# One of VectorE's three shifted arrays made by GpSimd in halves, in a fused attention and SwiGLU kernel

## The chip, the cores and the metric

The kernel runs on one core of a Trainium2 chip. A core has five engines, each with a queue of its own that runs in order: TensorE (PE, matrix products into PSUM), VectorE (DVE, elementwise work), ScalarE (ACT, exponentials and tanh), GpSimd (POOL, elementwise work on SBUF) and SyncE (SP, which here only issues DMAs). Engines meet through semaphores. The metric is the device time of one execution in microseconds (us); runs are repeated and the median is taken.

## The reference

One sequence of 2048 tokens, 512 channels. Multi-head attention with 32 heads of 16 channels and a SwiGLU feed-forward of width 1792 share the input and are mixed by a gate per token:

```
x = A_x                                              # 1 x 2048 x 512, bfloat16
g = sigmoid((x * gate_w).sum(-1, keepdims=True))
q, k, v = split(x @ wqkv)                            # 32 heads of 16
p = softmax(q k^T * 16 ** -0.5)                      # 32 x 2048 x 2048
a = (p v) @ wo
b = (silu(x @ w_gate) * (x @ w_up)) @ w_down
out = g * a + (1 - g) * b
```

The 32 x 2048 x 2048 = 134 million exponentials are what makes the kernel long.

## The kernel before

The scores are cut into 32 units (4 query blocks of 512 by 8 groups of 4 heads), each of 16 key blocks of 128. One key block of one unit is a tile: four heads, 128 keys by 512 queries each. Each tile's exponentials are made by one of two engines.

*By ScalarE.* `emit_pair` puts the scores of two heads (two matmuls that run side by side on different rows of TensorE) into one of two PSUM slots, `s_t`, and an ACTIVATE of 128 x 1024 with Exp writes `e_t`. A slot is free again when its exp has read it. A tile takes two such pairs.

*By VectorE.* `emit_d` lets one or two further score matmuls ride in the same round of TensorE, on rows that the pair leaves free, into a PSUM bank `d_t` (there are three such banks, which the other products share). `first` turns one head's scores into the bit pattern of an approximate exponential, a multiply and add that is stored as uint16 (128 x 512, the group `c_t<-d_t`); four of them make an array `y` of 128 x 2048. One such array is too coarse, so several are summed, and the sum is taken by the product with V. There are two ways. With `groups[n]` = 4, three further arrays are y plus one of three constants (`copy`, 128 x 2048 uint16, `SHIFTS`), four arrays in all. With `groups[n]` = 2, two bit operations (`bits`) and a multiplication (`product`, the TENSOR_TENSOR of 128 x 2048) make two arrays out of y. `quad` decides between them: 4 is taken when the planner has found idle time on TensorE of `SPARE` us. Arrays live in seven buffers ("homes"), which `home` hands out.

`pv` multiplies an array (or a tile's two `e_t`) with V: four matmuls of 512 columns on different columns of TensorE side by side, accumulated in the bank `o_ps`. All work of TensorE is of two modes: rows side by side (scores, "R") or columns side by side (the products with V, the projections and the feed-forward, "C"). Four or fewer matmuls that run side by side are called a round.

Everything else (projections, gate, feed-forward, output) is cut into chains of single rounds and is put between the exps by a `Pacer` with due times.

The order of every engine's instructions is fixed when the program is built. A planner keeps a time for each engine (`plan.pe`, `plan.act`, `plan.dve`), adds a cost for each instruction that it emits, and decides by these times what comes next. `spend` adds to TensorE's time, `spend_v` and `pay` to VectorE's. The main loop (`while au < UNITS`) looks at the room until the next `s_t` slot is free (`s_end`) and fills it with a product with V or a piece of a chain, else it emits the next pair. `fill_dve` does the same for VectorE: array pieces from PSUM that are due (`d_wait`), evictions (`owed`), and array work from SBUF to SBUF (`vops`). How many tiles go to VectorE comes out of this order: `v_unit` gives VectorE another tile when it could have it done in time. GpSimd works only at the start (clearing and filling constants).

All recorded instructions of TensorE carry the line of one helper (L164), those of ScalarE L167, those of VectorE and the DMAs L176, so groups are told apart by tile names.

Of the kernel before, what the change touches and what calls it, by code (L numbers as in the profile page):

```python
# [79 lines left out]
def kernel(  # L80
# [98 lines left out]
    queue = Ordered(nc.sync)  # L179

# [108 lines left out]
    class Plan:  # L289
        pe = dve = act = 0.0  # L290
# [11 lines left out]
    def spend(mode, mms, ready=0.0):  # L302

        plan.seq += 1
        work_at.append((plan.pe, mms))
        plan.pe = max(plan.pe + (0.1 if mode != plan.mode else 0.0), ready) + (0.226 if mode == "F" else 0.223) * mms
        plan.mode = mode

# [15 lines left out]
    def pay(i=0):  # L324
        ready, cost, f, c, key = owed.pop(i)
        spend_v(cost, ready, key)
# [21 lines left out]
    def m_tile(name):  # L348
# [3 lines left out]
        plan.pe = max(plan.pe, banks[i])  # L352
        banks[i] = None
        held[i] = ps_m[i].tile([P, QBW], F32, tag=f"m{i}", name=name)
        return held[i]
# [240 lines left out]
    def gate_end():  # L596
        act(out=ge[:, :], in_=ge[:, :], func=ACT.Exp, scale=-1.0)
        plan.act += 0.2
# [6 lines left out]
        later(0.5, end, plan.act + 0.2)  # L605
# [18 lines left out]
    w_gate, w_up, gs_of = {}, {}, {}  # L624
# [9 lines left out]
    def gu_chain(i):  # L634

        def gated(up):
            vec.scalar_tensor_tensor(out=mt[:, FS[i][1], :], in0=gs_of.pop(i)[:], scalar=0.5, in1=up[:, :],
                                     op0=ALU.mult, op1=ALU.mult)
            m_free(up, plan.dve)

        def gate(gp):
            th = work.tile([P, QBW], BF16, tag="th", name="th")
            flush_act(plan.pe + 0.4)
            act(out=th[:], in_=gp[:, :], func=ACT.Tanh, scale=0.5)
            plan.act = max(plan.act, plan.pe + 0.25) + 0.48
# [6 lines left out]
            later(0.6, f, plan.act + 0.25)  # L652

        cs = slice(FS[i][0] * QBW, (FS[i][0] + 1) * QBW)
        return [columns(DC, "gu", lambda dc, w=w: w[i][:, dc, :], lambda dc: xT[:, dc, cs], end)
                for w, end in ((w_gate, gate), (w_up, lambda p: later(0.6, lambda: gated(p))))]
# [34 lines left out]

    s_end = [0.0, 0.0]
# [4 lines left out]
    def emit_pair(bs, ride=0):  # L697
        i = pairs[0] % 2
        plan.pe = max(plan.pe + (0.1 if plan.mode != "R" else 0.0), s_end[i])
# [7 lines left out]
        for k in ride:  # L707
            emit_d(k)
        spend("R", 1)
        flush_act()  # L710
        ready = plan.pe + 0.27

        def exp():
            act(out=e_t[:], in_=s_t[:], func=ACT.Exp, scale=inv_sqrt_dh)
            plan.act = max(plan.act, ready) + ACT_US
            s_end[i] = plan.act + 0.2
            for b in bs:
                e_end[b] = plan.act + 0.27
        exps.append((ready, exp))
        for b in bs:  # L720
            e_left[b] = pairs[0]
        pairs[0] += 1

    exps = []
    ACT_US = 0.906
# [38 lines left out]
    def emit_d(i, rows=32):  # L764
# [7 lines left out]
        d_t = m_tile("d_t")  # L772
# [33 lines left out]
    def copy(n, k, i, y):  # L806
        h, c = home()
        vec.tensor_scalar(out=c, in0=y, scalar1=SHIFTS[k - 1], scalar2=None, op0=ALU.add)
        ready(n, k, h, c)
        if k == 3:  # L810
            drop(i, plan.dve + 0.2)
            y_live[0] -= 1

# [24 lines left out]
    def pay_v():  # L838
        cost, f, key, _, _ = vops.pop(0)
        spend_v(cost, 0.0, key)  # L840
        f()

    def fill_dve():

        while plan.dve <= plan.pe + 0.2:
            now = plan.dve
            due = [k for k, o in enumerate(owed) if o[0] <= now + 0.05]
            free = [k for k in due if owed[k][4] is None or owed[k][4] != plan.last]
            fit = bool(vops) and vops[0][3] // KT <= closed + AHEAD and c_ready() <= now
# [12 lines left out]
            elif fit:  # L862
                pay_v()
            elif d_wait or owed or vops and vops[0][3] // KT <= closed + AHEAD:
                t = min([w[0] for w in d_wait] + [o[0] for o in owed[:1]]
                        + [c_ready()] * bool(vops and vops[0][3] // KT <= closed + AHEAD))
                if t > plan.pe:
                    break
                plan.dve = max(plan.dve, t)
# [19 lines left out]
    def pv(n, k=None):  # L889

        un = n // KT
        if un not in o_of:
# [9 lines left out]
        if k is not None:  # L902
            c, slot = copies.pop((n, k))
        for i, b in enumerate(range(4 * n, 4 * n + 4)):
            j = HEADS[i]
            c0 = (4 * UNIT[un][1] + j) * VC
            mm(o[32 * j:32 * j + 32, :], lhsT=vaug[:, n % KT, c0:c0 + 32],
               rhs=e_of.pop(b) if k is None else c[:, i * QBW:(i + 1) * QBW],
               start=first, stop=last, tile_position=(0, 32 * j), skip_group_check=True)
            e_left.pop(b, None)  # L910
# [3 lines left out]
        spend("C", 1, 0.0 if k is not None else max(e_end.pop(b, 0.0) for b in range(4 * n, 4 * n + 4)))  # L914
# [194 lines left out]
    plan.dve = plan.pe + 3.9  # L1109

# [22 lines left out]
    def q0_again(p):  # L1133
# [4 lines left out]
        def scale():  # L1138
            act(out=ratio, in_=shift, func=ACT.Exp, scale=inv_sqrt_dh)
            plan.act += 0.48  # L1140
# [162 lines left out]
    def pv_list(now):  # L1303
# [14 lines left out]
        return r if early else [(n, k) for ready, n, k in vready if n // KT == un and (now is None or ready <= now and v_done(n))] + r  # L1318

    def emit_pv(item):  # L1320
        nonlocal closed
        un = closed
        pv(*item)
# [37 lines left out]
    def side(most):  # L1361
# [12 lines left out]
        if t is None or t > plan.pe or 0.226 * mms + (0.1 if plan.mode != mode else 0.0) > most:  # L1374
            return None
# [7 lines left out]
    def next_pv():  # L1383
        flush_act()
        while not pv_list(None):
            if d_wait:
                pay_d()
            elif vops and c_ready() < 1e9:
                pay_v()
            elif owed:  # L1390
# [9 lines left out]
    SLACK = 0.1  # L1400
    LEAD, LAST = 8.0, 6.0
    TILE_US = 1.87
# [31 lines left out]
    def quad():  # L1434
        if spare[0] > SPARE:
            spare[0] = 0.0
            return False
        return True

    def want_d():  # L1440
# [4 lines left out]
        open_ = sum(b is not None and b <= plan.pe for b in banks)  # L1445
# [4 lines left out]
    while au < UNITS:  # L1450
# [5 lines left out]
        back = pairs[0] - min(e_left.values(), default=pairs[0])  # L1456
        if back >= EB - 1:
# [3 lines left out]
        if room > 0.02:  # L1461
            n_pv = pv_list(plan.pe)
            switch = 0.0 if plan.mode == "C" else 0.1
# [3 lines left out]
            urgent = c is not None and c.deadline < 0 and back < EB - 4  # L1467
            visit = len(n_pv) + (len(c.pieces) - c.i if col else 0)
            going = col and 0 < c.i and len(c.pieces) < 6 and back < EB - 3
            if n_pv and fits > 0 and not urgent and not going and (plan.mode == "C" or visit > 1 and fits > 1 and (pv_turn[0] or c is None or col)  # L1470
                                      or back >= EB - 4 or (c is None or col) and fits == 1):
# [28 lines left out]
    while closed < UNITS or vops or vcur:  # L1500
# [26 lines left out]
    assert not vops and not vready and not vcur and not d_wait and not copies and au == closed == UNITS  # L1527
# [62 lines left out]
```

## Time and profile before

| | us |
|---|---|
| median of 3 runs | 773.16 (772.71 to 773.71) |
| profiled execution, its own time | 773.5 |
| its span (first to last instruction) | 771.7 |
| busy: TensorE / VectorE / ScalarE / GpSimd | 734.8 / 731.7 / 756.6 / 10.6 |
| exps of 128 x 1024 on ScalarE | 786 |
| tanh of 128 x 512 on ScalarE | 56, 40.9 busy |

[...] In the groups, the columns after the shapes are count, busy us and mean ns, then the idle time of the engine in front of the group and what ended it. In the waits: us in total, times, longest.

### The profile page before, as it was taken

To read this page: it belongs to the slowest core of one execution; us is meant where nothing else is said; L and a number is where in the kernel's file an instruction comes from. 1 tells how busy PE (TensorE), PEld (TensorE's weight loads), DVE (VectorE), ACT (ScalarE), POOL (GpSimd) and SP (SyncE) were. 2 spreads that over 40 slices of the span, in tenths; PEclk is the share of its full clock that TensorE was granted. 3 is DMA by queue.
4 is the path that set the end of the run, shared out by engine and by line. 5 is a ranking of instruction groups with operands and counts; after the bars stand their busy time and mean duration, and the time that the engine had idled before them with its cause. 6 is when DMAs were issued, how large, how long until landed. Compare 5 with 4: busy or idle time off the path is not lost.

```text
span 771.7 us, 21635 instructions
## 1 busy us (share of the span) xinstructions
PE 734.8 (95%) x8852; PEld 219.4 (28%) x8853; DVE 731.7 (95%) x1192; ACT 756.6 (98%) x855; POOL 10.6 (1%) x25
## 2 busy tenths in 40 slices
PE   8999999998999999999999999999999999999997
PEld 3322222222222222232222222222222232222222
DVE  6789999999989999999999999999999999999994
ACT  5999999999999999999999999999999999999996
POOL 5000000000000000000000000000000000000000
PEclk9999999999999999999999999999999999999999
DMA  8011303043210012220200221302000232100001
GB/s 191 2 19 39 69 16 77 21 122 85 48 43 12 14 41 64 65 46 21 50 15 15 51 72 36 75 21 55 19 12 25 61 78 58 30 19 11 16 28 35
DMA packets 91019, 34.36 MB, mean 45 GB/s; under 512 B 75488, under 2 KB 90472, under 8 KB 90920
## 3 DMA queue, kind: packets, MB, share of 16 engines
q1 hardware_dynamic: 89192, 32.66, 17.8%
q8 instruction: 69, 1.13, 0.6%
q10 hardware_dynamic: 1728, 0.33, 0.2%
q14 instruction: 30, 0.25, 0.1%
HBM read 21.55 MB, written 2.35 MB: 31 GB/s over the span
## 4 chain that ended last, share of the span: by engine, by line
ACT 45%; PE 34%; issue 11%; DVE 9%; DMA 0%; ACTq 0%; DVEq 0%
ACT e_t L167 42%; PE s_t L164 12%; PE o_ps L164 9%; DVE c_t L176 5%; PE gu L164 4%; ACT th L167 3%; PE ops L164 3%; PE qp L164 2%; PE vp L164 1%; PE kp L164 1%; PE dps L164 1%; DVE kaug L176 1%; DVE mt L176 1%; DVE gs L176 1%; PE warm L164 1%
## 5 line engine op out<-in xcount | busy, mean ns | idle before, releaser
L167 ACT ACTIVATE e_t<-s_t 128x1024 bf16<-128x1024 f32 x786 | 735.7, 1152 | 1.2 <-PE s_t L164 1.0
L176 DVE TENSOR_SCALAR c_t<-d_t 128x512 uint16<-128x512 f32 x396 | 262.6, 686 | 10.3 <-PE d_t L164 8.9
L164 PE MATMUL s_t<-qx,kaug 32*128 32x512 bf16 (+1 forms) x1240 | 241.7, 382 | 21.5 <-ACT e_t L167 19.3
L164 PEld LDWEIGHTS <-kaug 32*128 32x128 bf16 (+1 forms) x2048 | 95.7, 91 | 339.3 <-issue 335.4
L164 PE MATMUL o_ps<-e_t,vaug 128*32 128x512 bf16 x1572 | 152.3, 386 | 0.1
L164 PE MATMUL d_t<-qx,kaug 32*128 32x512 bf16 x392 | 138.5, 384 | 0.0
L176 DVE TENSOR_SCALAR c_t<-c_t 128x2048 uint16<-128x2048 uint16 x193 | 130.0, 688 | 0.8
L164 PE MATMUL o_ps<-c_t,vaug 128*32 128x512 bf16 x1096 | 101.9, 385 | 0.5 <-DVE osb L176 0.2
L164 PEld LDWEIGHTS <-vaug 128*32 128x32 bf16 (+1 forms) x2856 | 61.8, 94 | 99.7 <-issue 92.1
L164 PE MATMUL gu<-xT,wg 128*32 128x512 bf16 x896 | 72.4, 384 | 0.0
L176 DVE TENSOR_TENSOR c_t<-c_t 128x2048 bf16<-128x2048 bf16 x59 | 71.9, 1218 | 0.0
L164 PE MATMUL gu<-xT,wu 128*32 128x512 bf16 x896 | 69.2, 383 | 0.1
L164 PE MATMUL ops<-wd_t,mt 128*32 128x512 bf16 x672 | 56.4, 382 | 0.0
L176 DVE TENSOR_SCALAR kaug<-d_t 128x512 uint16<-128x512 f32 x72 | 48.0, 686 | 2.7 <-PE d_t L164 2.7
L164 PE MATMUL s_t<-q,kaug 32*128 32x512 bf16 (+1 forms) x196 | 38.2, 382 | 5.0 <-ACT e_t L167 4.6
L167 ACT ACTIVATE th<-gu 128x512 bf16<-128x512 f32 x56 | 40.9, 731 | 0.0
L176 DVE SCALAR_TENSOR_TENSOR gs<-th,gu 128x512 bf16<-128x512 bf16 x56 | 38.3, 683 | 2.7 <-ACT th L167 2.6
L176 DVE SCALAR_TENSOR_TENSOR mt<-gs,gu 128x512 bf16<-128x512 bf16 x56 | 38.3, 684 | 1.6
L164 PEld LDWEIGHTS <-mt 128*32 128x32 bf16 (+1 forms) x1037 | 24.4, 95 | 27.9 <-issue 21.9
L176 DVE TENSOR_SCALAR c_t<-kaug 128x2048 uint16<-128x2048 uint16 x43 | 29.1, 689 | 0.1
L164 PEld LDWEIGHTS <-wu 128*32 128x32 bf16 x896 | 18.9, 95 | 25.5 <-issue 17.4
L164 PEld LDWEIGHTS <-wg 128*32 128x32 bf16 x896 | 17.6, 94 | 24.9 <-issue 21.7
(141 smaller groups left out, 439.9 us busy)
## 6 DMA issues: line engine op xcount, KB each, us to landing
wg<-in_B_w_gate_dram SPq DMA_DIRECT2D x56, 128.0 KB
wu<-in_B_w_up_dram SPq DMA_DIRECT2D x56, 128.0 KB
on<-osb SPq DMA_DIRECT2D x120, 16.0 KB
rb<-rr SPq DMA_DIRECT2D x15, 128.0 KB
wd_t<-in_B_w_down_dram SPq DMA_DIRECT2D x7, 256.0 KB
qx<-qst SPq DMA_DIRECT2D x96, 16.0 KB
qx<-aq SPq DMA_DIRECT2D x96, 16.0 KB
out_dram<-o_t SPq DMA_DIRECT2D x12, 128.0 KB
```

Source lines behind the costliest of these rows:

```text
L164: return ordered(nc.tensor.matmul(*args, **kw))
L167: ordered(nc.scalar.activation(*args, **kw))
L176: return lambda *a, **kw: ordered(f(*a, **kw))
```

## The change

Of an array set with `groups[n]` = 4, the third shifted array is no longer queued in `vops` when a new list `gq` has a place (two at most). Its work is done in two halves of 1024 columns by `g_half`, either on GpSimd or on VectorE. `g_now` runs whenever VectorE's next instruction is chosen: if at least two (`GNEED`) reads of PSUM are waiting for VectorE, it emits a half on GpSimd, with a wait on the VectorE instruction emitted last. Until the planned end of that half (`plan.lock`), `fill_dve` holds back operations from SBUF to SBUF: those of `vops`, and entries of `owed` that cost under 0.45 (`wide`). When VectorE has nothing else, `g_dve` does a half there.

```diff
+                todo[n] = 3
-                for k in range(1, 4):
+                for k in range(1, 4 - (len(gq) < GQ)):
                     vops.append((0.6, lambda k=k: copy(n, k, h, y), ("y", n) if k == 1 else None, n, True))
+                if len(gq) < GQ:
+                    gq.append([n, h, y, [0, 1], None])
...
+    def g_half(engine, now):
+        g = gq[0]
+        n, h, y, left, c = g
+        if c is None:
+            c = g[4] = home()
+        half = left.pop(0)
+        cols = slice(half * GHALF, (half + 1) * GHALF)
+        before = last_of.get(nc.vector.engine)
+        ins = engine.tensor_scalar(out=c[1][:, cols], in0=y[:, cols], scalar1=SHIFTS[2], scalar2=None, op0=ALU.add)
+        if engine is gps:
+            if before is not None:
+                tc.add_manual_dep(ins.ins, before.name,
+                                  mybir.DependencyInfo(mybir.DependencyClass.Sync, mybir.DependencyReason.DATA),
+                                  reason="beside reads of PSUM")
+            t = plan.pool = plan.lock = max(plan.pool, now + 0.12) + 1.13
+        else:
+            t = plan.dve
+        if not left:
+            gq.pop(0)
+            vready.append((t + 0.3, n, 3))
+            copies[n, 3] = (c[1].bitcast(BF16), c[0])
+            copied(n, h, t)
+
+    def g_now(now):
+        while gq and gq[0][0] // KT <= closed + AHEAD and plan.pool <= now + 0.1 and (gq[0][4] is not None or min(c_free) <= now):
+            soon = sum(d[0] <= now + 0.05 + 0.6 * i for i, d in enumerate(d_wait)) + sum(o[0] <= now + 0.05 and not wide(o[1]) for o in owed)
+            if soon < GNEED:
+                return
+            g_half(gps, now)
+
+    def g_dve():
+        if gq[0][4] is None:
+            plan.dve = max(plan.dve, min(c_free))
+        spend_v(0.335, plan.lock)
+        g_half(vec, plan.dve)
```

A product with V may be cut by columns: where the room in front of the next slot is too short for a whole round, `pv` takes as many quarters of the 512 columns as fit, and the rest comes first at the next chance.

```diff
-    def pv(n, k=None):
+    def pv(n, k=None, most=QBW):
...
+        c0 = cut.pop("done", 0)
+        c1 = min(QBW, c0 + most)
+        cols = slice(c0, c1)
...
+        share = (c1 - c0) / QBW
+        if c1 < QBW:
+            cut.update(item=(n,) if k is None else (n, k), done=c1)
+            spend("C", share, 0.0 if k is not None else max(e_end[b] for b in range(4 * n, 4 * n + 4)))
+            return
...
+            part_cols = int((room + SLACK - switch) / 0.217 * CUTS) * QBW // CUTS
+            if n_pv and plan.mode == "C" and part_cols > 0 and may_cut():
+                emit_pv(n_pv[0], part_cols)
+                continue
```

Four arrays instead of two are taken in more cases, and the planner's figures are set anew (those not shown change in the same way: the tanh, the gate's exps, and the banks that a riding score may take):

```diff
-        plan.pe = max(plan.pe + (0.1 if mode != plan.mode else 0.0), ready) + (0.226 if mode == "F" else 0.223) * mms
+        plan.pe = max(plan.pe + (FLIP if mode != plan.mode else 0.0), ready) + (0.226 if mode == "F" else 0.217) * mms
...
-        ready = plan.pe + 0.27
+        ready = plan.pe + 0.38
...
-            s_end[i] = plan.act + 0.2
+            s_end[i] = plan.act + SLOT
             for b in bs:
-                e_end[b] = plan.act + 0.27
+                e_end[b] = plan.act + 0.06
...
+    FLIP = 0.107
+    SLOT = 0.05
-    ACT_US = 0.906
+    ACT_US = 0.9167
...
-        d_wait.append((plan.pe + 0.5, first, n))
+        d_wait.append(((end[0] if end else plan.pe) + 0.28, first, n))
...
     def quad():
-        if spare[0] > SPARE:
+        if sum(f < 1e9 for f in c_free) < FREE4:
+            return True
+        if spare[0] > SPARE or EAGER(len(GQL()), back[0]):
             spare[0] = 0.0
             return False
         return True
+    FREE4 = 2
+    EAGER = lambda q, b: q == 0 and b <= 4
...
-    SLACK = 0.1
+    SLACK = 0.16
+    CUTS = 4
...
-    TILE_US = 1.87
+    TILE_US = 1.9
```

(In `quad`, False means four arrays.) What the two programs contain, where they differ:

| | before | after |
|---|---|---|
| exps of 128 x 1024 (ScalarE) | 786 | 774 |
| tiles on VectorE: four arrays / two | 41 / 78 | 61 / 64 |
| pieces of 128 x 512 from PSUM (VectorE) | 476 | 500 |
| operations on a whole array of 2048, one input (VectorE) | 279 | 250 |
| products of 2048 (VectorE) | 78 | 64 |
| half copies of 1024: VectorE / GpSimd | 0 / 0 | 23 / 99 |
| products with V, in full rounds | 713 | 759 |
| of them cut in two | 0 | 55 |
| changes of mode on TensorE | 1509 | 1503 |

More of the change, by code (lines that the diff above doesn't have):

```diff
@@ L325, in pay @@
         ready, cost, f, c, key = owed.pop(i)
-        spend_v(cost, ready, key)
+        spend_v(cost, max(ready, plan.lock) if wide(cost) else ready, key)
         keep, plan.chain = plan.chain, None
@@ L604, in end @@
             vec.reciprocal(odds[:, :], ge[:, :])
-        later(0.5, end, plan.act + 0.2)
+        later(0.5, end, plan.act + 0.05)
     def turn_odds():
@@ L651, in f @@
                 gs_of[i] = gs
-            later(0.6, f, plan.act + 0.25)
+            gs_at[i] = plan.act + 0.05
+            later(0.6, f, gs_at[i])
         cs = slice(FS[i][0] * QBW, (FS[i][0] + 1) * QBW)
         return [columns(DC, "gu", lambda dc, w=w: w[i][:, dc, :], lambda dc: xT[:, dc, cs], end)
-                for w, end in ((w_gate, gate), (w_up, lambda p: later(0.6, lambda: gated(p))))]
+                for w, end in ((w_gate, gate), (w_up, lambda p: later(0.6, lambda: gated(p), max(plan.pe + 0.25, gs_at[i]))))]
     scaled = set()
@@ L698, in emit_pair @@
         i = pairs[0] % 2
-        plan.pe = max(plan.pe + (0.1 if plan.mode != "R" else 0.0), s_end[i])
+        plan.pe = max(plan.pe + (FLIP if plan.mode != "R" else 0.0), s_end[i])
         plan.mode = "R"
@@ L706, in emit_pair @@
             e_of[b] = e_t[:, k * QBW:(k + 1) * QBW]
[L707 to L708 removed]
         spend("R", 1)
         flush_act()
[L711 removed]
+        ready = plan.pe + 0.38
+        for k in ride:
+            emit_d(k, riding=True)
         def exp():
@@ L771, in emit_d @@
         left.remove(i)
-        d_t = m_tile("d_t")
+        end = []
+        d_t = m_tile("d_t", end if riding else None)
         score(d_t[:, :], 4 * n + i, rows)
@@ L809, in copy, with copied @@
         ready(n, k, h, c)
-        if k == 3:
-            drop(i, plan.dve + 0.2)
-            y_live[0] -= 1
+        copied(n, i, plan.dve)
+    def copied(n, i, t):
+        todo[n] -= 1
+        if not todo[n]:
+            drop(i, t + 0.2)
+            y_live[0] -= 1
+    todo = {}
+    gq = []
+    GQ = 2
+    GHALF = NV * QBW // 2
+    def g_half(engine, now):
[13 more added lines that the diff above has]
+            t = plan.pool = plan.lock = max(plan.pool, now + 0.12) + 1.13
+        else:
+            t = plan.dve
[10 more added lines that the diff above has]
+            g_half(gps, now)
+    GNEED = 2
+    def g_dve():
[3 more added lines that the diff above has]
+        g_half(vec, plan.dve)
     def bits(n, k, y):
@@ L839, in pay_v @@
         cost, f, key, _, _ = vops.pop(0)
-        spend_v(cost, 0.0, key)
+        spend_v(cost, plan.lock, key)
         f()
@@ L846, in fill_dve @@
             now = plan.dve
-            due = [k for k, o in enumerate(owed) if o[0] <= now + 0.05]
+            g_now(now)
+            shut = locked(now)
+            due = [k for k, o in enumerate(owed) if o[0] <= now + 0.05 and not (shut and wide(o[1]))]
             free = [k for k in due if owed[k][4] is None or owed[k][4] != plan.last]
-            fit = bool(vops) and vops[0][3] // KT <= closed + AHEAD and c_ready() <= now
+            fit = bool(vops) and not shut and vops[0][3] // KT <= closed + AHEAD and c_ready() <= now
             if fit and vops[0][3] // KT < au and vops[0][2] != plan.last:
@@ L863, in fill_dve @@
                 pay_v()
+            elif gq and not shut and gq[0][0] // KT <= closed + AHEAD and (gq[0][4] is not None or min(c_free) <= now) and (len(gq) == GQ or not d_wait):
+                g_dve()
             elif d_wait or owed or vops and vops[0][3] // KT <= closed + AHEAD:
-                t = min([w[0] for w in d_wait] + [o[0] for o in owed[:1]]
-                        + [c_ready()] * bool(vops and vops[0][3] // KT <= closed + AHEAD))
+                t = min([w[0] for w in d_wait] + [max(o[0], plan.lock if wide(o[1]) else 0.0) for o in owed[:1]]
+                        + [max(c_ready(), plan.lock)] * bool(vops and vops[0][3] // KT <= closed + AHEAD))
                 if t > plan.pe:
                     break
-                plan.dve = max(plan.dve, t)
+                plan.dve = max(plan.dve + 0.03, t)
                 plan.last = None
@@ L902, in pv @@
         if k is not None:
-            c, slot = copies.pop((n, k))
+            c, slot = copies[n, k]
         for i, b in enumerate(range(4 * n, 4 * n + 4)):
             j = HEADS[i]
-            c0 = (4 * UNIT[un][1] + j) * VC
-            mm(o[32 * j:32 * j + 32, :], lhsT=vaug[:, n % KT, c0:c0 + 32],
-               rhs=e_of.pop(b) if k is None else c[:, i * QBW:(i + 1) * QBW],
+            v0 = (4 * UNIT[un][1] + j) * VC
+            e = e_of[b] if k is None else c[:, i * QBW:(i + 1) * QBW]
+            mm(o[32 * j:32 * j + 32, cols], lhsT=vaug[:, n % KT, v0:v0 + 32], rhs=e[:, cols],
                start=first, stop=last, tile_position=(0, 32 * j), skip_group_check=True)
-            e_left.pop(b, None)
+        share = (c1 - c0) / QBW
[3 more added lines that the diff above has]
+            return
+        cut.clear()
+        if k is not None:
+            copies.pop((n, k))
+        else:
+            for b in range(4 * n, 4 * n + 4):
+                e_of.pop(b)
+                e_left.pop(b, None)
         pvs[un] += 1
@@ L913, in pv @@
             later(0.6, take_part, plan.pe + 0.47)
-        spend("C", 1, 0.0 if k is not None else max(e_end.pop(b, 0.0) for b in range(4 * n, 4 * n + 4)))
+        spend("C", share, 0.0 if k is not None else max(e_end.pop(b, 0.0) for b in range(4 * n, 4 * n + 4)))
         if k is None:
@@ L1317, in pv_list, with may_cut, emit_pv @@
         r = [(n,) for n in r]
-        return r if early else [(n, k) for ready, n, k in vready if n // KT == un and (now is None or ready <= now and v_done(n))] + r
-    def emit_pv(item):
+        r = r if early else [(n, k) for ready, n, k in vready if n // KT == un and (now is None or ready <= now and v_done(n))] + r
+        item = cut.get("item")
+        return r if item is None else [item] + [i for i in r if i != item]
+    def may_cut():
+        return closed and pvs[closed] and pv_left(closed) > 3
+    def emit_pv(item, most=QBW):
         nonlocal closed
         un = closed
-        pv(*item)
+        pv(item[0], item[1] if len(item) > 1 else None, most)
+        if cut:
+            return
         if len(item) > 1:
@@ L1373, in side @@
         t = m_ready(int(takes)) if takes else 0.0
-        if t is None or t > plan.pe or 0.226 * mms + (0.1 if plan.mode != mode else 0.0) > most:
+        if t is None or t > plan.pe or 0.226 * mms + (FLIP if plan.mode != mode else 0.0) > most:
             return None
@@ L1389, in next_pv @@
                 pay_v()
+            elif gq and (gq[0][4] is not None or min(c_free) < 1e9):
+                g_dve()
             elif owed:
@@ L1444, in want_d @@
         one = c is not None and c.pieces[c.i][2] and (pace.credit > 0 or c.deadline <= plan.slot + 4)
-        open_ = sum(b is not None and b <= plan.pe for b in banks)
+        open_ = sum(b is not None and b <= max(plan.pe, s_end[pairs[0] % 2]) + BANK_WAIT for b in banks)
         if not d_wait and len(vops) < 2:
@@ L1455 @@
         flush_act(plan.pe)
-        back = pairs[0] - min(e_left.values(), default=pairs[0])
-        if back >= EB - 1:
+        back[0] = pairs[0] - min(e_left.values(), default=pairs[0])
+        if back[0] >= EB - 1:
             next_pv()
@@ L1462 @@
             n_pv = pv_list(plan.pe)
-            switch = 0.0 if plan.mode == "C" else 0.1
+            switch = 0.0 if plan.mode == "C" else FLIP
             fits = int((room + SLACK - switch) / 0.216)
@@ L1466 @@
             col = c is not None and (c.pieces[c.i][3:] or "C")[0] == "C"
-            urgent = c is not None and c.deadline < 0 and back < EB - 4
+            urgent = c is not None and c.deadline < 0 and back[0] < EB - 4
             visit = len(n_pv) + (len(c.pieces) - c.i if col else 0)
-            going = col and 0 < c.i and len(c.pieces) < 6 and back < EB - 3
+            going = col and 0 < c.i and len(c.pieces) < 6 and back[0] < EB - 3
             if n_pv and fits > 0 and not urgent and not going and (plan.mode == "C" or visit > 1 and fits > 1 and (pv_turn[0] or c is None or col)
-                                      or back >= EB - 4 or (c is None or col) and fits == 1):
+                                      or back[0] >= EB - 4 or (c is None or col) and fits == 1):
                 emit_pv(n_pv[0])
@@ L1526 @@
         pay()
-    assert not vops and not vready and not vcur and not d_wait and not copies and au == closed == UNITS
+    assert not vops and not gq and not vready and not vcur and not d_wait and not copies and au == closed == UNITS
     assert not at
```

34 lines of the change are left out of this document (24 added, 10 removed).

## The prediction

> **What bounds the kernel now.** I read the page's busy table first, then the chain, the costliest groups, and the waits.
>
> ```profile
> span 771.7 us, 21635 instructions
> ...
> PE 734.8 (95%) x8852; PEld 219.4 (28%) x8853; DVE 731.7 (95%) x1192; ACT 756.6 (98%) x855; POOL 10.6 (1%) x25
> ...
> ACT 45%; PE 34%; issue 11%; DVE 9%; DMA 0%; ACTq 0%; DVEq 0%
> ...
> L167 ACT ACTIVATE e_t<-s_t 128x1024 bf16<-128x1024 f32 x786 | 735.7, 1152 | 1.2 <-PE s_t L164 1.0
> L176 DVE TENSOR_SCALAR c_t<-d_t 128x512 uint16<-128x512 f32 x396 | 262.6, 686 | 10.3 <-PE d_t L164 8.9
> ...
> L176 DVE TENSOR_SCALAR c_t<-c_t 128x2048 uint16<-128x2048 uint16 x193 | 130.0, 688 | 0.8
> ...
> L176 DVE TENSOR_TENSOR c_t<-c_t 128x2048 bf16<-128x2048 bf16 x59 | 71.9, 1218 | 0.0
> ```
>
> Three engines are nearly full, but only ScalarE (ACT) is never without work: its 786 exps show 1.2 us of idle in front of them. The waits say the same from the other side, and a stretch of the timeline shows the beat:
>
> ```profile
> PE s_t L164 <- ACT e_t L167: 24.9, 71, 0.8
> ...
> ACT e_t L167 <- PE s_t L164: 1.0, 3, 0.5
> ```
>
> ```profile
> 302.86 7.55 ACT L167 ACTIVATE e_t<-s_t 128x1024 bf16<-128x1024 f32 x8
> ...
> 306.91 0.39 PE L164 MATMUL s_t<-qx,kaug 32*128 32x512 bf16 x2
> ...
> 307.23 0.62 PE L164 MATMUL o_ps<-e_t,vaug 128*32 128x512 bf16 x8
> ...
> 307.78 0.39 PE L164 MATMUL s_t<-qx,kaug 32*128 32x512 bf16 x2
> ```
>
> TensorE (PE) waits for ScalarE 71 times, 24.9 us; ScalarE waits for TensorE 3 times, 1.0 us. An exp's record is 1.152 long but overlaps the next: eight take 7.55, so (7.55 - 1.15)/7 = 0.914 from start to start. Over the trace's 727 exp-to-exp steps the starts are 0.920 apart in the mean and 0.904 in the median, which is also the least. The excess, 727 x 0.016 = 11.5 us, is exps that start a little late because their scores came late. The first exp starts at 13.6 and the last ends at 763.6: the end of the kernel is the sum of those steps plus 8.1 us of tail. So the term that counts is the number of exps.
>
> **The change, part by part.** Counts are those of the two built programs.
>
> *ScalarE.* 786 exps become 774; tanh stays at 56. Twelve steps of 0.920 fall out: -11.0 us, if the mean lateness stays. Without any lateness the 774 exps need 774 x 0.904 + 56 x 0.478 (the step from a tanh to the next exp) = 726.5 us, before 737.3.
>
> *TensorE.* The 12 pairs of key blocks (six tiles of four) go to VectorE, and more of VectorE's tiles use four arrays instead of two: 61 of 125 after, 41 of 119 before. Each array is one more product with V, four matmuls of 512 columns side by side, one round. Rounds of this kind go from 1650 to 1696, counted in full widths. A round is 0.217 by the trace's steps within a run; the stretch above (one score round, two rounds, the next score) is 0.87 = 3 x 0.217 + 2 changes of mode, so 0.109 a change. Sum: +46 x 0.217 = +10.0; 12 score rounds less, -2.6; 1503 changes of mode instead of 1509, -0.7: +6.7 us. The 55 products cut into 384 and 128 columns (or the like) are priced by the nearest row, the four 128-column rounds of the tail:
>
> ```profile
> 765.53 0.41 PE L164 MATMUL rps<-ident,rt 128*32 128x128 bf16 x16
> ```
>
> They start 0.055 to 0.066 apart, a quarter of 0.217 (0.054): a cut costs 0 to 0.012, 0.7 us at most; I take 0. TensorE's rounds and mode changes were 1650 x 0.217 + 786 x 0.217 + 1509 x 0.109 = 693 us under ScalarE's 737.3 and become 700 under 726.5. It stays below, but the margin falls from 44 to 27 us. That margin is what hides the +6.7; without it they would all be on the path.
>
> *VectorE.* The steps from start to start in the trace are 0.601 for an array piece from PSUM (`c_t<-d_t`), 0.599 for a whole copy of 2048, 1.134 for a product, 0.199 for 512 columns from SBUF (`aq<-qst`), so about 0.33 for 1024. 24 more pieces: +14.4; 29 copies less: -17.4; 14 products less (78 to 64): -15.9; 23 half copies that remain here: +7.7. Sum -11.2. Count times lower-decile step, summed over all kinds, was 715 us and becomes 704; the tail's stretch included, VectorE runs from 0.9 to 768.4.
>
> *GpSimd.* New are 99 adds of a constant on 1024 uint16 columns (the rest of 61 third arrays), each behind a wait on the VectorE instruction emitted before it. What is queued behind such a wait on GpSimd is only the next half; TensorE's product with that array waits for it, and VectorE when it overwrites a buffer. No row shows this operation. The nearest are these:
>
> ```profile
> L508 POOL MEMSET q<- 128x1024 bf16 x1 | 1.0, 954 | 0.0
> ...
> L260 POOL TENSOR_SCALAR_AFFINE_SELECT ident<-ident 128x128 bf16<-128x128 bf16 x1 | 0.3, 292 | 0.0
> ...
> L276 POOL MEMSET sel_t<- 128x4 bf16 x1 | 0.1, 104 | 0.0
> ```
>
> The memset writes 1024 columns but reads nothing: lower end 0.95. The select reads, compares and writes 128 in 0.292, of which 0.104 is the fixed part: 0.104 + 8 x 0.188 = 1.61 for 1024, upper end. An add with one input is nearer to the memset, with a read stream beside the write: I take 1.1.
>
> Does a half hold up VectorE? No row of this trace shows the two together (GpSimd is idle after the start-up). Bounds: nothing, or all VectorE work from SBUF to SBUF stands still until the half is done. I take the second. In the built program 44 of the 99 halves are followed by two VectorE reads of PSUM before the next SBUF-to-SBUF operation, 30 by three or more, 23 by one, 2 by none; a read covers 0.60. With 0.1 to start, 1.1 holds for 1.2: 2 x 1.2 + 23 x 0.6 = 16 us of standing (12.5 at 0.95; 51 at 1.61; 0 without a hold). VectorE then has 704 + 16 = 720 us in a stretch of some 756, before 715 in 767: idle 36 instead of 52. That idle is the cover; it holds.
>
> [...]
>
> *The planner's figures* (mode change 0.1 to 0.107, round 0.223 to 0.217, exp 0.906 to 0.9167, tanh, and when scores, slots and arrays are ready) set the order only. From the end of a pair's score round to the reuse of its slot they add up to 0.27 + 0.906 + 0.2 = 1.376 before, 0.38 + 0.917 + 0.05 = 1.347 after. In the trace an exp that follows at once starts 0.49 after its last score matmul's start (0.27 after the round), and slots are taken 1.10 to 1.20 after the exp's start: about 1.39. Bounds: -0.03 x 774 = 23 us of TensorE standing before a slot, all within its 27 us of margin; or, where the order fits better, up to the 11.5 us of lateness saved. I take 0. SP's queue keeps its 584 entries and nothing is moved past a DMA.
>
> Sum: 771.7 - 11.0 = 760.7 span; the profiled execution's own 773.5 becomes 762.5. The median 773.16 lies 0.3 lower, so **762.1 us**, -1.4%. A measurement of this kernel tells 0.2% (1.5 us) from no change.
>
> **Rivals.**
>
> 1. *GpSimd too slow, so VectorE becomes the bound (slower).* With a half of length L held for h = L + 0.1, the standing is 2h + 23(h - 0.6) + 44(h - 1.2) for h up to 1.8. VectorE's 704, that, and the idle it cannot fill (first 50 us: 12; last 22 us: 11; from the stretch table) make 771.7 when the standing is 45 us: h = 1.61, L = 1.51. From there each 0.1 us costs 7 us: 780 at 1.61, 795 at 1.8. For: the select's row reaches 1.61, and 25 halves have one cover or none. Against: the memset at 0.95. A harder form: every VectorE operation stands still for each half, 99 x 1.1 = 109, so 704 + 109 + 23 = 836. [...] Together 0.23, of which 0.03 for the harder form.
>
> 2. *TensorE too tight.* Lateness grows as its margin shrinks: 11.5 x 44/27 = 18.7, +7.2, so 769. For: the margin; against: no score was late by more than 0.5 us before. 0.14.
>
> 3. *The new figures make TensorE stand before slots* with its other work behind it, and the gain is spent: 12 us of the 23 reach the exps, 773. For: 1.347 against 1.39; against: the margin. 0.06.
>
> 4. *The order fits better.* Half of the lateness goes: 11 + 5.8, so 756. For: the round and mode figures now equal the trace's 0.217 and 0.109, and cuts of 128 columns fill the 0.035 between 0.87 and 0.904; against: lateness is spread evenly over the span (0.6 to 1.0 us in every 50), which names no single fault. 0.07.
>
> That the change does nothing is excluded by the counts.
>
> **How the numbers follow.** Forecast 0.50 (757 to 767), rival 1 0.23, 2 0.14, 3 0.06, 4 0.07. Faster by over 0.2%: 0.50 + 0.14 + 0.07 = 0.71; same 0.06; slower 0.23. The range reaches from rival 4's middle, 755, to 782, past the length of 1.61: below is left out some 0.03, above some 0.12.
>
> **What would show it.** Right: 774 exps, 0.915 to 0.925 from start to start; ScalarE's idle before exps still 1 to 2 us; halves of 0.95 to 1.3 us; copies of 2048 mostly at 0.69 with a few tens stretched by half a microsecond; VectorE's busy share not above 96%. Wrong: exps that wait for TensorE by many microseconds; halves of 1.5 us or more, or PSUM reads stretched beside them; waits of TensorE for `c_t` made by GpSimd.

## The result, and the profile after

The changed kernel takes 826.4 us (824.0 to 829.1, 5 runs) against 773.0 (772.6 to 773.7): a ratio of 1.069 with an interval of 1.067 to 1.071. 762.1 was forecast, 755 to 782 the range. Chance 0.23 stood on the slower side.

The page of the changed kernel, its lines that answer to those before:

```profile
span 824.7 us, 22621 instructions
...
PE 759.3 (92%) x9256; PEld 221.7 (27%) x9257; DVE 749.3 (91%) x1196; ACT 756.0 (92%) x843; POOL 296.2 (36%) x124
...
PE 38%; DVE 29%; POOL 16%; ACT 11%; issue 5%; DMA 1%; POOLq 0%; SPq 0%; DVEq 0%; ACTq 0%
...
L167 ACT ACTIVATE e_t<-s_t 128x1024 bf16<-128x1024 f32 x774 | 729.3, 1066 | 54.2 <-PE d_t L164 26.5
L176 POOL TENSOR_SCALAR c_t<-c_t 128x1024 uint16<-128x1024 uint16 x79 | 227.6, 2888 | 421.5 <-DVE c_t L176 252.8
L176 DVE TENSOR_SCALAR c_t<-d_t 128x512 uint16<-128x512 f32 x428 | 281.1, 681 | 29.2 <-PE d_t L164 25.9
...
L164 PE MATMUL o_ps<-c_t,vaug 128*32 128x512 bf16 (+2 forms) x1352 | 132.0, 375 | 37.4 <-POOL c_t L176 34.2
...
L176 DVE TENSOR_SCALAR c_t<-c_t 128x2048 uint16<-128x2048 uint16 (+1 forms) x189 | 136.6, 736 | 1.9 <-PE o_ps L164 0.6
```

The row that decides is GpSimd's: a half takes 2.89 us in the mean (least 2.76, median 2.77), where 1.1 was counted. The other rows follow from it, as the experiments show. TensorE's products with V stand idle for 34.2 us, waiting for arrays of GpSimd; before, they waited for VectorE alone, and hardly at all:

```profile
L164 PE MATMUL o_ps<-c_t,vaug 128*32 128x512 bf16 x1096 | 101.9, 385 | 0.5 <-DVE osb L176 0.2 <-DVE c_t L176 0.2
```

ScalarE, which had stood 1.2 us before its exps, stands 54.2. In the chain ScalarE falls from 45% to 11% and GpSimd appears with 16%. No engine is full any more: 92, 91 and 92%. They wait for one another in turn.

The sum, from the first exp to the last: 750.0 us before, 802.4 after. Twelve steps of 0.904 less are -10.8. The excess of the exps' steps over 0.904 grows from 11.5 to 69.9, +58.4 (the mean step is 1.002 where 0.920 was forecast); the step from a tanh to the next exp grows from 0.478 to 0.568, 56 of them, +5.0. Together +52.6, measured +52.4.

One such place, in the timeline of the changed kernel (start, length, what; in brackets idle time in front and what ended it):

```profile
296.53 6.06 POOL L176 TENSOR_SCALAR c_t<-c_t 128x1024 uint16<-128x1024 uint16 x2 [5.24 <-DVE c_t L176]
...
300.45 0.38 PE L164 MATMUL o_ps<-c_t,vaug 128*32 128x512 bf16 x2
302.64 0.51 PE L164 MATMUL o_ps<-c_t,vaug 128*32 128x512 bf16 x2 [1.82 <-POOL c_t L176]
...
303.09 0.60 PE L164 MATMUL s_t<-q,kaug 32*128 32x512 bf16 x2
...
303.77 0.69 DVE L176 TENSOR_SCALAR kaug<-d_t 128x512 uint16<-128x512 f32 x1 [2.07 <-PE d_t L164]
303.80 1.02 ACT L167 ACTIVATE e_t<-s_t 128x1024 bf16<-128x1024 f32 x1 [2.21 <-PE d_t L164]
```

Two halves of one array take 6.06 us. TensorE does two of the four matmuls of its product at 300.45 (their columns are in the first half) and waits 1.82 for the others. All later scores stand behind them in its queue, so ScalarE (2.21) and VectorE (2.07) run dry too. The planner counts 1.13 for a half, 2.26 for the two.

### The profile page after: what moved, and what is told of

Read it like the earlier page. It is cut to its first block, busy times and chain, and to the rows that moved or that the text cites. A ratio compares the mean times of both kernels' runs of the same rounds, so it can differ in the third digit from the quotient of the medians.

```text
span 824.7 us, 22621 instructions
## 1 busy us (share of the span) xinstructions
PE 759.3 (92%) x9256; PEld 221.7 (27%) x9257; DVE 749.3 (91%) x1196; ACT 756.0 (92%) x843; POOL 296.2 (36%) x124
## 4 chain that ended last, share of the span: by engine, by line
PE 38%; DVE 29%; POOL 16%; ACT 11%; issue 5%; DMA 1%; POOLq 0%; SPq 0%; DVEq 0%; ACTq 0%
DVE c_t L176 19%; POOL c_t L176 14%; PE s_t L164 12%; PE o_ps L164 11%; ACT e_t L167 10%; PE gu L164 5%; DVE kaug L176 3%; PE ops L164 3%; DVE mt L176 2%; PE qp L164 2%; DVE gs L176 1%; POOL kaug L176 1%; PE dps L164 1%; DVE osb L176 1%; PE kp L164 1%
## 5 line engine op out<-in xcount | busy, mean ns | idle before, releaser
L167 ACT ACTIVATE e_t<-s_t 128x1024 bf16<-128x1024 f32 x774 | 729.3, 1066 | 54.2 <-PE d_t L164 26.5
L176 POOL TENSOR_SCALAR c_t<-c_t 128x1024 uint16<-128x1024 uint16 x79 | 227.6, 2888 | 421.5 <-DVE c_t L176 252.8
L164 PE MATMUL o_ps<-c_t,vaug 128*32 128x512 bf16 (+2 forms) x1352 | 132.0, 375 | 37.4 <-POOL c_t L176 34.2
L164 PE MATMUL o_ps<-e_t,vaug 128*32 128x512 bf16 (+2 forms) x1668 | 156.2, 373 | 0.0
L176 DVE TENSOR_SCALAR c_t<-c_t 128x2048 uint16<-128x2048 uint16 (+1 forms) x189 | 136.6, 736 | 1.9 <-PE o_ps L164 0.6
L164 PEld LDWEIGHTS <-vaug 128*32 128x32 bf16 x3260 | 73.7, 95 | 167.4 <-issue 155.4
L176 DVE TENSOR_TENSOR c_t<-c_t 128x2048 bf16<-128x2048 bf16 x42 | 50.9, 1212 | 0.0
L176 POOL TENSOR_SCALAR kaug<-c_t 128x1024 uint16<-128x1024 uint16 x9 | 26.5, 2948 | 46.4 <-DVE c_t L176 46.4
L164 PE MATMUL s_t<-q,kaug 64*128 64x512 bf16 (+1 forms) x188 | 37.8, 399 | 1.4 <-ACT e_t L167 1.2
L176 POOL TENSOR_SCALAR c_t<-kaug 128x1024 uint16<-128x1024 uint16 x9 | 25.6, 2855 | 30.2 <-DVE aq L176 10.6
L176 DVE TENSOR_SCALAR kaug<-c_t 128x2048 uint16<-128x2048 uint16 (+1 forms) x42 | 31.7, 757 | 1.0 <-PE o_ps L164 0.6
```

What stands on the lines that cost most here:

```text
L164: return ordered(nc.tensor.matmul(*args, **kw))
L167: ordered(nc.scalar.activation(*args, **kw))
L176: return lambda *a, **kw: ordered(f(*a, **kw))
```

## The experiments

All times are beside the kernel before on the same chip, where it took 772.7 to 773.0. The labels stand for: e1 a clearing in place of the addition, e5 the addition by itself, e6 another form of the addition, e9 no wait of TensorE, e8 and e14 a delay, e2 the planner told the length, e4 the same order with VectorE, e3 no GpSimd, e10 and e12 variants of e6. Three theories stood at the start: only the length of the half was wrong (A); the new figures and the cut products make TensorE too tight (B); VectorE's work stretches what GpSimd does (C).

**The same order with a short half (e1).**

```diff
-        ins = engine.tensor_scalar(out=c[1][:, cols], in0=y[:, cols], scalar1=SHIFTS[2], scalar2=None, op0=ALU.add)
+        if engine is gps:
+            ins = gps.memset(c[1][:, cols].bitcast(BF16), 0.0)
+        else:
+            ins = engine.tensor_scalar(out=c[1][:, cols], in0=y[:, cols], scalar1=SHIFTS[2], scalar2=None, op0=ALU.add)
```

> Each of the 99 GpSimd halves is replaced by a clearing of the same 1024 columns, in the same place of the same order (this leaves out the addition: the third array of those tiles is zero there). A clearing of this size took 0.951 before, an addition 2.77 after. Theory A (the half lasts 2.77 us where 1.1 was counted, and everything lost comes from that): the sum of the prediction comes back, 760 to 768 us, exps 0.915 to 0.93 apart, no waits of TensorE for arrays of GpSimd. Rival B (the new figures and the cut products make TensorE too tight): above 785 us, exps still 0.97 or more apart. Rival C (VectorE's work beside it stretches whatever GpSimd does): the clearings last well over 1 us too, and the time is above 785.

763.1 us, ratio 0.9875 (0.986 to 0.989). The clearings took 0.951, as in the start-up. Its groups on GpSimd and on ScalarE:

```profile
L176 POOL MEMSET c_t<- 128x1024 bf16 x90 | 85.6, 951 | 574.0 <-DVE c_t L176 332.3 <-PE d_t L164 66.1 <-PE s_t L164 29.8
```

```profile
L167 ACT ACTIVATE e_t<-s_t 128x1024 bf16<-128x1024 f32 x774 | 722.3, 1104 | 1.1 <-PE s_t L164 0.8 <-ACT e_t L167 0.2
```

ScalarE's idle is 1.1 us again, its step 0.920, and from the first exp to the last it takes 739.3, where the forecast's 750.0 - 11.0 gives 739.0. B falls: with every other instruction in place, the order gives what was forecast. So does C for a clearing.

**The addition by itself (e5).** Behind the start-up work of the kernel before, GpSimd works on a spare tile: in uint16 it adds a constant, and in bfloat16 and float32 it multiplies by a constant with the same instruction. Then it copies, and adds two int32 tensors.

```diff
+    for n in (1024, 512, 256, 1024, 512, 256):
+        nc.gpsimd.tensor_scalar(out=pb[:, 0:n], in0=pa[:, 0:n], scalar1=94.0, scalar2=None, op0=ALU.add)
+    for n in (1024, 512):
+        nc.gpsimd.tensor_scalar(out=pb[:, 0:n].bitcast(BF16), in0=pa[:, 0:n].bitcast(BF16), scalar1=2.0, scalar2=None, op0=ALU.mult)
...
+    for n in (512, 256):
+        nc.gpsimd.tensor_tensor(out=pb[:, 0:2 * n].bitcast(I32), in0=pa[:, 0:2 * n].bitcast(I32), in1=pa[:, 0:2 * n].bitcast(I32), op=ALU.add)
```

> The kernel before, with additions of a constant put behind GpSimd's start-up work: uint16 of 1024, 512 and 256 columns twice, and other forms (bfloat16, float32, a copy, int32 with two inputs), to measure the half by itself. Theory A: uint16 of 1024 lasts 2.7 to 2.8 also here, and 512 about half of it and a fixed part: some 1.5. Rival C: about 1.1 where VectorE does nothing from SBUF to SBUF beside it. The time of the kernel stays 773 within 2 us.

The groups of GpSimd in that run:

```profile
L519 POOL TENSOR_SCALAR pa<-pa 128x1024 uint16<-128x1024 uint16 x2 | 5.6, 2780 | 0.2
L519 POOL TENSOR_SCALAR pa<-pa 128x512 uint16<-128x512 uint16 x2 | 3.0, 1488 | 0.2
L521 POOL TENSOR_SCALAR pa<-pa 128x1024 bf16<-128x1024 bf16 x1 | 2.8, 2773 | 0.1
...
L519 POOL TENSOR_SCALAR pa<-pa 128x256 uint16<-128x256 uint16 x2 | 1.7, 847 | 0.2
...
L523 POOL TENSOR_SCALAR pa<-pa 128x512 f32<-128x512 f32 x1 | 1.5, 1488 | 0.1
L525 POOL COPY pa<-pa 128x1024 uint16<-128x1024 uint16 x1 | 1.0, 1037 | 0.1
L528 POOL TENSOR_TENSOR pa<-pa 128x512 int32<-128x512 int32 x1 | 1.0, 1037 | 0.1
```

0.85, 1.49 and 2.78 for 256, 512 and 1024: 0.2 us fixed and 2.5 ns an element, the same for the addition in uint16 and the multiplication in bfloat16 and float32. So 2.77 is the price of this operation and not of what stands beside it; C falls. A copy of the same 1024 columns takes 1.04, and so does an addition of two int32 tensors of 512 elements, which are the same bytes (both inputs are one tile here).

**The same order, the whole computation, in the faster form (e6).** Two uint16 columns are added at once: the tile `twice` holds 94 in both halves of each int32.

```diff
+    twice = const.tile([P, 512], I32, name="twice")
+    nc.gpsimd.memset(twice[:], 94.0 * 65537)
...
-        ins = engine.tensor_scalar(out=c[1][:, cols], in0=y[:, cols], scalar1=SHIFTS[2], scalar2=None, op0=ALU.add)
+        if engine is gps:
+            ins = gps.tensor_tensor(out=c[1][:, cols].bitcast(I32), in0=y[:, cols].bitcast(I32), in1=twice[:, :], op=ALU.add)
+        else:
+            ins = engine.tensor_scalar(out=c[1][:, cols], in0=y[:, cols], scalar1=SHIFTS[2], scalar2=None, op0=ALU.add)
```

> The whole computation, in the order of the changed kernel; only the form of the 99 halves on GpSimd is another: two uint16 columns are added at once as one int32 (512 elements and a constant tile with the number in both halves). This form lasted 1.037 us in the run that measured forms. Theory A (only the length of the half was wrong): 760 to 768 us, 774 exps 0.915 to 0.93 apart. [...]

766.7 us, ratio 0.9918 (0.9903 to 0.9933), faster than both kernels and inside A's bounds.

```profile
L176 POOL TENSOR_TENSOR c_t<-c_t,twice 128x512 int32<-128x512 int32 x79 | 100.4, 1272 | 501.1 <-DVE c_t L176 266.2 <-PE d_t L164 74.6 <-PE s_t L164 48.1
```

```profile
L167 ACT ACTIVATE e_t<-s_t 128x1024 bf16<-128x1024 f32 x774 | 723.1, 1085 | 2.0 <-PE s_t L164 0.9 <-ACT e_t L167 0.2
```

With two different inputs a half takes 1.27, 0.32 more than the clearing. What the 3.5 us above e1 come from was not settled. Between e6 and the changed kernel only the form of 99 instructions differs (and the constant tile): those 1.5 us a half cost 59.7 us of time.

**What the longer half costs, and where (e9, e8, e14).** Two theories are set against each other: A1, most of the loss is TensorE waiting for late arrays; A2, most of it is VectorE standing still beside the halves. In e9 the uint16 halves stay, and TensorE waits for none of them:

```diff
-            copies[n, 3] = (c[1].bitcast(BF16), c[0])
+            copies[n, 3] = (xT[:, 0, :], c[0])
```

> The uint16 halves stay (2.77 us each), but TensorE's product with the third array of those tiles reads a tensor that is always there (the third array's part is left out of the result and replaced by another), so it waits for no half. What stays is VectorE's standing beside the halves and the buffers that come free late. Theory A1: 770 to 790 us. Theory A2: 805 to 830 us.

784.9 us, ratio 1.016 (1.014 to 1.018), inside A1's bounds. So of the 59.7 us, 41.5 go when TensorE waits for no half, and 18.2 stay. Busy times in e6, then in e9:

```profile
PE 736.5 (96%) x9257; PEld 220.6 (29%) x9257; DVE 726.2 (95%) x1196; ACT 748.3 (98%) x843; POOL 136.8 (18%) x125
```

```profile
PE 746.0 (95%) x9257; PEld 220.3 (28%) x9257; DVE 745.6 (95%) x1196; ACT 754.2 (96%) x843; POOL 296.5 (38%) x124
```

VectorE's busy time in e9 is 19.4 us above e6's and near the changed kernel's 749.3: its work is stretched almost as much as there, and the kernel is 41.5 us shorter all the same. The 18.2 are about those 19.4, so they are put down to VectorE held beside the halves; that was not tried by itself.

The other two runs were to add only lateness. In e8, 17 clearings of 4 columns stand in front of each int32 half; in e14, 44 behind it, and then one of the last 4 columns of the half.

```diff
+            for k in range(17):
+                w = gps.memset(late[:, 4 * k:4 * k + 4], 0.0)
...
+            for k in range(44):
+                gps.memset(late[:, 4 * (k % 16):4 * (k % 16) + 4], 0.0)
+            gps.memset(c[1][:, cols][:, GHALF - 4:].bitcast(BF16), 0.0)
```

> [...] Theory A1 (the loss of 63 us is mostly the late arrays, awaited by TensorE and filling GpSimd's queue): 805 to 830 us. Theory A2 (mostly VectorE standing still): 765 to 785 us.

> The int32 halves in the order of the changed kernel; behind each half GpSimd clears 4 columns of a spare tile 44 times (33 ns apart by the run before) and then the last 4 of the half's 1024 columns, which are left out of the result so. VectorE is held by the half as planned, but the array is ready some 1.5 us later, about when a uint16 half would have been. Theory A1 (most of the loss is TensorE waiting for late arrays): 795 to 815 us, against 766.7 without the delay. Theory A2 (late arrays cost little where nothing is held): 767 to 780 us.

798.6 and 859.2 us: both outside the bounds of either theory, and neither tells what it was meant to. In e8 the clearings came 33 ns apart and delayed the half by 0.55 only, where 1.8 was reckoned with (an estimate: 17 x 0.104, the clearing of 4 columns in the kernel before). The stretch in which VectorE is held moved by as much, partly out of its cover: the 250 copies of 2048 take 0.80 in the mean, against 0.70 in e6. e14, slower than the changed kernel itself, shows why on VectorE:

```profile
154.85 1.27 POOL L176 TENSOR_TENSOR c_t<-c_t,twice 128x512 int32<-128x512 int32 x1 [3.47 <-DVE c_t L176]
156.05 1.44 POOL L176 MEMSET late<- 128x4 bf16 x44
157.42 0.11 POOL L176 MEMSET c_t<- 128x4 bf16 x1
```

```profile
155.29 0.68 DVE L176 TENSOR_SCALAR c_t<-d_t 128x512 uint16<-128x512 f32 x1
155.89 2.18 DVE L176 TENSOR_SCALAR c_t<-c_t 128x2048 uint16<-128x2048 uint16 x1
157.99 0.67 DVE L176 SCALAR_TENSOR_TENSOR mt<-gs,gu 128x512 bf16<-128x512 bf16 x1
```

A copy of 0.69 that begins at 155.89 ends at 158.07, 0.54 after the last clearing: here a train of tiny clearings held a copy as one long operation does. Reads of PSUM beside it keep their 0.67 to 0.68. So lateness alone, with no hold, was not measured, and the 41.5 rest on e9 alone.

**Telling the planner (e2), VectorE instead (e4), no GpSimd (e3).** In e2 the uint16 halves stay and the planner is told their length:

```diff
-            t = plan.pool = plan.lock = max(plan.pool, now + 0.12) + 1.13
+            t = plan.pool = max(plan.pool, now + 0.12) + 2.77
+            plan.lock = t - 1.87
```

> The addition stays; the planner is told that a half takes 2.77 us and that VectorE is held for its first 0.9. 84 halves on GpSimd, 30 on VectorE, 774 exps. Theory A: the arrays are no longer awaited too early, which is most of the loss, but the second held stretch still meets VectorE unplanned: 768 to 790 us. Rival B: above 800 us. Rival C: halves of more than 2.77 in the mean and above 800 us.

782.1 us, 1.011 (1.010 to 1.013): most of the loss goes, but the order is still slower than before. In e4 the halves are done by VectorE in the same places.

```diff
-        ins = engine.tensor_scalar(out=c[1][:, cols], in0=y[:, cols], scalar1=SHIFTS[2], scalar2=None, op0=ALU.add)
+        ins = vec.tensor_scalar(out=c[1][:, cols], in0=y[:, cols], scalar1=SHIFTS[2], scalar2=None, op0=ALU.add)
...
-            if before is not None:
+            if False:
```

> The order of everything else is kept; the 99 halves are done by VectorE where GpSimd had them (0.335 each, 33 us more for VectorE: 704 + 33 = 737 of step time). Theory A: no hold and arrays ready in time, but a fuller VectorE: 770 to 795 us. Rival B: the loss stays, 815 us or more. Rival C: as A.

785.5 us, 1.016 (1.015 to 1.018): even 33 us more for VectorE cost less than halves of 2.77 us. In e3 nothing goes to GpSimd, and the new rule that takes four arrays more often (`EAGER`) is off.

```diff
-    GQ = 2
+    GQ = 0
...
-    GQL = lambda: gq
+    GQL = lambda: [0]
```

> No work for GpSimd: all third arrays are whole copies on VectorE, four arrays are taken by the old rule alone; the planner's figures and the cut products stay. 780 exps, 78 products of 2048, 288 copies. By the prediction's terms: 6 steps of 0.920 less than before, 773 - 5.5 = 767.5, 764 to 771 if the new figures cost no lateness; 773 or more if they do.

769.2 us, 0.995 (0.994 to 0.997). So 3.6 of e6's gain of 6.2 us come without any work on GpSimd, in an order of 780 exps with the new figures and the cuts. The step is 0.922 there.

**Two variants of e6.** e10 plans the half at 1.25; e12 besides lets GpSimd begin when one read of PSUM waits.

```diff
-            t = plan.pool = plan.lock = max(plan.pool, now + 0.12) + 1.13
+            t = plan.pool = plan.lock = max(plan.pool, now + 0.12) + 1.25
...
-    GNEED = 2
+    GNEED = 1
```

> The int32 form, and the planner's length of a half set from 1.13 to 1.25 (it lasted 1.27 there, 0.12 of it counted apart). 776 exps, 89 halves on GpSimd, 25 on VectorE. Arrays and holds are then planned as they come: two steps of 0.920 more than the int32 run, less lateness: 764 to 768 us; below 766 if the 0.14 by which the halves ran over was what cost it its 3.5 us against the clearing.

> As the run with the length told, and a half is given to GpSimd already when one read of PSUM waits for VectorE instead of two: 774 exps, 141 halves on GpSimd, 1 on VectorE, 71 four-array tiles. More work leaves VectorE, but more holds have no cover. If the cover of two reads matters: 768 to 778 us; if not: 761 to 766 us.

772.2 us, 0.999 (0.998 to 1.000), and 769.4, 0.995 (0.994 to 0.996). The first misses its bounds; the second lies in those for a cover that matters. But two exp steps in e10 are 3.23 and 4.27 us long, 5.7 more than two of 0.904; e12 has one of 5.98, 5.1 more; e6 has none over 1.37. Without these steps the times would be some 766.5 and 764.3 (an estimate, 772.2 - 5.7 and 769.4 - 5.1): inside the first's 764 to 768, and inside the bounds for a cover that does not matter. At the longest in e10 TensorE waits at the end of a unit, first for GpSimd (0.17), then for VectorE's eviction of `o_ps` (0.84) and for an array of VectorE's (0.73), with no score emitted between. This looks like a property of the built order and not of the price of a half, so the two runs say little about planning at 1.25 or about a cover of one read.

## Why the prediction was wrong

**The step that failed** is the price of a half: "An add with one input is nearer to the memset, with a read stream beside the write: I take 1.1", with 0.95 and 1.61 as its ends. It is 2.77 in the kernel and 2.78 alone. Neither row carried over. The select's 0.292 for 128 columns, scaled, gave 1.47 ns an element; the addition takes 2.5, and by e5's line its 128 columns would take 0.2 + 0.32 = 0.52 (an estimate). The upper end was another operation's price, scaled by a factor of eight, and was not a bound.

**The rest of the sum held**, as e1 shows with a half of 0.95: 763.1 against 762.1. The 774 exps and the mean step of 0.920 (measured 0.920) need no correction. VectorE's 11.2 us less agree too (busy 731.7 before, 720.0 in e1). TensorE's +6.7 us and the cuts at nothing were not measured one by one; with a short half they do not reach the end. The hold of VectorE, 16 us of standing, was an assumption that no row of the kernel before shows; it was priced too high, without harm: no copy is stretched in e1, where 12.5 us were counted at 0.95, and in e6 the copies and products of 2048 are stretched by some 5 us in all (250 copies at 0.703 and 64 products at 1.229 in the mean, in e1 0.687 and 1.217).

**Rival 1 had the cause and the side**: GpSimd too slow, deciding from a half of 1.51. Two of its steps were off. It saw VectorE become the bound, while VectorE's busy share fell from 95% to 91% and the larger part, 41.5 of 59.7 us by e9, came by TensorE. The prediction had named that path ("TensorE's product with that array waits for it") and priced it at nothing, since at 1.1 the order covers it. And the hold does not last as long as the half. In the changed kernel 98 copies of 2048 begin beside a half. Five begun 0.37 to 0.7 us after its start end at 1.58, 0.9 + 0.69; 61 begun 0.93 to 1.75 take their 0.68 or 0.69; 28 begun from 1.75 on end 0.55 behind the half; four begun in its last 0.07 take 0.68. A half, then a copy of the second kind beside it and one of the first kind beside another half:

```profile
107.00 2.77 POOL L176 TENSOR_SCALAR c_t<-c_t 128x1024 uint16<-128x1024 uint16 x1 [0.23 <-DVE aq L176]
```

```profile
108.14 0.69 DVE L176 TENSOR_SCALAR c_t<-wd_t 128x2048 uint16<-128x2048 uint16 x1
...
122.69 1.21 DVE L176 TENSOR_SCALAR c_t<-c_t 128x2048 uint16<-128x2048 uint16 x1
```

The half beside the second copy begins at 122.32. So a half holds VectorE's copies for its first 0.9 us and its last 0.9, and leaves some 0.85 between in which a copy can begin. A copy begun late in that part puts off the second hold: such halves end 0.89 after the copy, which is why the mean is 2.89 and the median 2.77. With the int32 form it is otherwise: in e6, 36 of 42 copies begun inside a half end 0.55 after its end, the others begin in its last 0.12. PSUM reads go on beside the halves: an array piece takes 0.681 in the mean after, 0.686 before, and the 134 pieces of `c_t<-d_t` that lie wholly inside a half take 0.679, at most 0.693. The harder form of the rival, everything standing still, falls by the same row. Moving this work from VectorE to GpSimd lost time in one form (826.4 us) and gained in the other (766.7).

**Rivals 2 and 3** fall with e1, which keeps the order, the figures and the cuts. **Rival 4**, a better order, did not come either: the step is 0.920 in e1.

**The cover of two reads** (44 halves with two, 30 with more) fits an operation of 1.13, which is the planner's figure. The int32 form holds a copy until some 1.13 after its start (an estimate from e6: 1.27 + 0.55 - 0.69).

## What to carry to other kernels

Before an operation that the trace does not show is moved to another engine, measure it there by itself, in the very form and size; rows of other operations on that engine did not bound it here. In an order that is fixed beforehand, a wrong length costs through every queue that waits in order behind it: 1.5 us more on 99 instructions of GpSimd, which is busy for 36% of the span, cost 60 us. And when a slow form is found, look for the same bytes in another type or operation before giving the idea up.

## What was not expected of the hardware

The granted clock of TensorE falls to 0.50 in six stretches of the changed kernel, of 3.4 us each. The stretches around the wait shown above (us; busy time and count of PE, PEld, DVE, ACT and POOL; then the granted clock, the DMA share and GB/s):

```profile
297.00:300.40 3.40, 3.40 (x50) 0.93 (x45) 3.40 (x5) 3.40 (x5) 3.40 (x2) 1.00 0.09 23
300.40:302.60 2.20, 0.43 (x6) 0.00 (x0) 1.30 (x3) 1.19 (x2) 2.19 (x1) 1.00 0.63 149
302.60:306.40 3.80, 3.76 (x28) 0.74 (x27) 2.54 (x4) 1.69 (x2) 0.00 (x0) 0.55 0.00 0
306.40:309.00 2.60, 2.60 (x39) 0.87 (x36) 1.38 (x3) 2.60 (x4) 0.00 (x0) 1.00 0.06 13
```

The granted clock is 0.55 in the 3.8 us after a stand of 1.8 (0.50 from 302.8 to 306.2), and a round takes about 0.43 there instead of 0.217. Not every stand is followed by such a stretch: after one of 2.2 us at 179.0 the clock stays at 1.00. Over the span the granted clock is 0.988, and 1.000 before: 1.2% of 824.7 is about 10 us of TensorE's work (an estimate), so part of what e9 takes away may be this (e9's clock is 1.0). That share was not tried by itself.

On GpSimd, an operation with one input and a constant takes 2.5 ns an element (an addition in uint16, a multiplication in bfloat16 and float32), a copy of 1024 uint16 1.04 us in all, and an addition of two int32 inputs from one tile 1.037 us for 512 elements and 0.672 for 256, (1.037 - 0.672) / 256 = 1.4 ns an element. Even with two different inputs 512 int32 take 1.27 us (e6), while 512 uint16 and a constant take 1.49.
